# The second batch's output projection as seven block products for eight in two of three groups

## The chip, the cores and the metric

The kernel runs on one core of a Trainium2 chip. TensorE (PE) multiplies matrices, VectorE (DVE) and ScalarE (ACT) work element by element, SyncE (SP) issues the transfers. The metric is the device time of one execution in microseconds (us), the median of several. Arithmetic is float32; every weight or activation that PE sees is split into a high and a low part, and three matmuls (high x high, high x low, low x high) stand for one product.

## The reference

Two batches of 768 tokens pass through a banded attention with block summaries, and then through two layers:

```python
x = attention(q, k, v)                             # 1536 tokens x 512
x = (sigmoid(x @ w_gate) * (x @ w_val)) @ w_out    # 512 -> 1536 -> 512
h = max(x @ w1, x @ w2, x @ w3)                    # 512 -> 768
return h @ w_out2                                  # 768 -> 512
```

The change is in the product with `w_out` in the second line, for the second batch.

## The kernel before, in words

The hidden width of the first layer, 1536, is cut into 12 blocks of 128 columns (`f`), four to a group, three groups (`g`). A batch's 768 tokens are two halves of 384 (`a`), the free size of one matmul.

Batch 0 computes gate and value by plain products (`make_A`), then multiplies by `w_out` group by group (`make_B`): for each token half and each of four 128-wide output blocks (`dm`) 4 x 3 matmuls into one PSUM bank, whose sum is then copied (first group) or added (the others) to `y` in SBUF. The attention of batch 1 runs between these.

Batch 1 computes gate and value in `make_Q`, as block products: a pair of hidden blocks (`j`, six pairs), two halves of the contraction and two token halves make a 2 x 2 block product that takes seven products instead of eight (numbers 1 to 7, Strassen's scheme in Winograd's form: `FORMS` names the operand of each). A product is six matmuls of 384 columns. The weight operands are made by `blocks` (four sums on DVE) and `split` (a cast on ACT, a subtraction on DVE); the activation operands by `make_forms`. After a group's four gate and value products the projection of that group follows, by `make_B` in the plain form, 96 matmuls. The results of a group's products leave PSUM through DVE and ACT, are multiplied (gate x value) and split into the operands `h`. The second layer (`make_P`) uses block products again for both batches, and `make_D` ends the program.

The weights of batch 0 are kept in DRAM as they are converted (`keep`) and read back for batch 1 (`again`, one tile `w` of 128 x 1024 for each hidden block of `w_out`). There are ten `w` buffers, nine `h`, eight large `x`, and PSUM banks in two sets of four, `m` and `s`.

The order of every engine's instructions is made beforehand, by `Plan`: each task has an engine, a duration, a due time and the tasks that it follows; a list scheduler places them, twice refined, and the program is written in that order. The list `acc` fixes PE's order of the groups, the due times follow from it, and `chain["acc"]` keeps it.

## Time and profile before

| | |
|---|---|
| runs | 539.06, 540.60, 541.69 us; median 540.6 |
| profiled execution | 539.13 us, of which the span of its instructions is 537.4 us |
| busy share of the span | PE 98%, DVE 78%, ACT 56% |
| mean granted clock of PE | 0.997 |

Busy time is the union of an engine's instructions. Matmuls overlap, so the start of one block product to the start of the next is the better measure of PE's pace than the duration of a matmul. DVE instructions overlap a little as well. A wait is put down to whoever released it last.

### The profile page before, as it was taken

Reading aid. Unit: us, or ns where it says so; the run is one execution under the profiler, and the core shown is the slowest. Engines: PE = TensorE matmul, PEld = TensorE weight load, DVE = VectorE, ACT = ScalarE, POOL = GpSimd, SP = SyncE. Lnnn points to the kernel's source line nnn. Section 1 sums busy time; section 2 is a strip of 40 time slices with the busy share of each in tenths; the row PEclk is TensorE's granted clock in tenths of the full one; section 3 lists DMA queues with packets and bytes.
Section 4 is the critical chain, followed back from the end, with each engine's and each line's share of the span. In section 5 each row is a group of like instructions: output and inputs, shape, how many; then the busy total and the mean of one; then the engine's idle time right before and its main releaser. Section 6 shows DMA issues by size and latency. Waiting matters only on the chain.

```text
span 537.4 us, 10140 instructions
## 1 busy us (share of the span) xinstructions
PE 528.9 (98%) x3850; PEld 503.8 (94%) x3850; DVE 419.1 (78%) x988; ACT 303.5 (56%) x724; POOL 4.5 (1%) x22
## 2 busy tenths in 40 slices
PE   7999999999999999999999999999999999999997
PEld 5788999999999999999999999999999999998886
DVE  5899996999898358895389589999999998995000
ACT  5899986678656684664466167354434344463111
POOL 3000000000000000000000000000000000000000
PEclk9899999999999999999999999999999999999999
DMA  8999898969666010161143037102222223201121
GB/s 279 302 336 372 298 342 267 303 237 374 206 210 235 13 40 0 41 234 40 41 148 127 10 105 278 45 36 61 96 79 79 79 88 110 78 1 41 59 79 59
DMA packets 28128, 78.25 MB, mean 146 GB/s; under 512 B 3504, under 2 KB 6960, under 8 KB 28080
## 3 DMA queue, kind: packets, MB, share of 16 engines
q1 hardware_dynamic: 24960, 73.87, 40.5%
q10 hardware_dynamic: 3120, 3.74, 2.1%
q8 instruction: 30, 0.49, 0.4%
q14 instruction: 18, 0.15, 0.1%
HBM read 61.28 MB, written 15.73 MB: 143 GB/s over the span
## 4 chain that ended last, share of the span: by engine, by line
PE 87%; DVE 7%; DMA 2%; ACT 1%; issue 1%; SPq 1%; ACTq 0%
PE m L923 19%; PE m L884 14%; PE s L1017 12%; PE m L1017 12%; PE m L1217 9%; PE m L1116 8%; PE s L1116 8%; PE s L792 2%; DMA vn<-in_vn_dram 1%; PE s L747 1%; PE s L779 1%; DMA raw<-in_wts_dram 1%; DVE c L503 1%; DVE e L754 1%; SPq L630 1%
## 5 line engine op out<-in xcount | busy, mean ns | idle before, releaser
L884 PE MATMUL m<-x,w 128*128 128x384 f32 x576 | 108.6, 340 | 1.0 <-ACT t L901 0.8
L923 PE MATMUL m<-h,w 128*128 128x384 f32 x576 | 105.4, 336 | 0.0
L884 PEld LDWEIGHTS m<-x,w 128*128 128x128 f32 x576 | 98.7, 188 | 3.5 <-ACT t L901 1.3
L923 PEld LDWEIGHTS m<-h,w 128*128 128x128 f32 x576 | 99.6, 188 | 0.4 <-DVE y L947 0.2
L1017 PE MATMUL m<-x,w 128*128 128x384 f32 x294 | 56.1, 334 | 0.0
L1017 PE MATMUL s<-f,w 128*128 128x384 f32 x294 | 56.0, 334 | 0.0
L1017 PEld LDWEIGHTS m<-x,w 128*128 128x128 f32 x294 | 51.5, 188 | 0.1
L1017 PEld LDWEIGHTS s<-f,w 128*128 128x128 f32 x294 | 51.4, 188 | 0.1
L1116 PE MATMUL s<-f,w 128*128 128x384 f32 x252 | 48.1, 335 | 0.2 <-ACT t L1131 0.2
L1116 PE MATMUL m<-f,w 128*128 128x384 f32 x252 | 46.8, 335 | 0.0
L1116 PEld LDWEIGHTS s<-f,w 128*128 128x128 f32 x252 | 43.9, 188 | 0.6 <-ACT t L1131 0.5
L1116 PEld LDWEIGHTS m<-f,w 128*128 128x128 f32 x252 | 43.9, 188 | 0.2 <-ACT tc L1131 0.2
L760 ACT ACTIVATE e<-e,nm 128x120 f32<-128x120 f32 x96 | 36.6, 384 | 6.9 <-DVE nm L754 6.8
L435 ACT ACTIVATE w<-c 128x512 fp32r<-128x512 f32 (+1 forms) x50 | 29.3, 588 | 19.4 <-DVE c L503 12.6
L438 DVE TENSOR_TENSOR w<-raw,w 128x512 fp32r<-128x512 f32 (+1 forms) x48 | 28.6, 619 | 13.7 <-ACT w L435 13.6
L435 ACT ACTIVATE h<-t 128x384 fp32r<-128x384 f32 x48 | 24.6, 523 | 17.5 <-DVE t L1156 14.5
L499 DVE SCALAR_TENSOR_TENSOR c<-raw,c 128x512 int32<-128x512 int32 x50 | 34.2, 685 | 0.3
L503 DVE SCALAR_TENSOR_TENSOR c<-raw,c 128x512 int32<-128x512 int32 x50 | 34.1, 684 | 0.3
L435 ACT ACTIVATE w<-raw 128x512 fp32r<-128x512 f32 (+1 forms) x48 | 25.8, 571 | 14.7 <-PE m L923 11.1
L438 DVE TENSOR_TENSOR w<-c,w 128x512 fp32r<-128x512 f32 (+1 forms) x50 | 31.8, 639 | 1.9 <-ACT w L435 1.6
L438 DVE TENSOR_TENSOR h<-t,h 128x384 fp32r<-128x384 f32 x48 | 26.4, 554 | 6.6 <-ACT h L435 6.2
L1032 ACT ACTIVATE tc<-s 128x384 f32<-128x384 f32 x27 | 13.3, 491 | 27.8 <-PE s L1017 27.7
(137 smaller groups left out, 798.7 us busy)
## 6 DMA issues: line engine op xcount, KB each, us to landing
raw<-in_wts_dram SPq DMA_DIRECT2D x60, 512.0 KB, 4.2
kept_o<-w SPq DMA_DIRECT2D x12, 512.0 KB, 5.7
w<-kept_o SPq DMA_DIRECT2D x12, 512.0 KB, 5.0
k<-in_kn_dram SPq DMA_DIRECT2D x8, 400.0 KB, 7.1
q<-in_qt_dram SPq DMA_DIRECT2D x16, 192.0 KB, 6.9
v<-in_vw_dram SPq DMA_DIRECT2D x16, 192.0 KB, 5.6
raw<-kept_g SPq DMA_DIRECT2D x6, 512.0 KB, 3.1
raw<-kept_v SPq DMA_DIRECT2D x6, 512.0 KB, 4.4
```

The lines of the kernel that those rows point to most:

```text
L435: nc.scalar.activation(out=dst, in_=src, func=ACTF.Copy)
L438: nc.vector.tensor_tensor(out=dst, in0=src, in1=h.bitcast(F32), op=ALU.subtract)
L499: nc.vector.scalar_tensor_tensor(out=c.t, in0=half(r, 1), scalar=-0x40000000, in1=c.t, op0=ALU.bitwise_and, op1=ALU.bitwise_or)
L503: nc.vector.scalar_tensor_tensor(out=c.t, in0=half(r, 0), scalar=29, in1=c.t, op0=ALU.logical_shift_right, op1=ALU.bitwise_or)
L760: nc.scalar.activation(out=e[h].t[:, t], in_=e[h].t[:, t], func=ACTF.Exp, scale=-1.0, bias=nm.t[:, h, t:t + 1], accum_out=sm.t[:, h, t:t + 1])
L792: nc.tensor.matmul(px.t[64 * h:64 * h + 64, c:c + 64], lhsT=vt.t[:, t, par, h], rhs=at[h].t[0:CW, t, 64 * par:64 * par + 64], start=True, ...
L884: nc.tensor.matmul(ps.t, lhsT=w.t.rearrange("p s (k f) -> p s k f", k=KC)[:, wh, kc], rhs=src[kc // 2].t[:, xh, kc % 2], start=(kc == 0 an ...
L923: nc.tensor.matmul(ps.t, lhsT=w.t.rearrange("p s (k f) -> p s k f", k=KC)[:, wh, dm], rhs=h.t[:, xh], start=(i == 0 and j == 0), stop=(i = ...
L1017: nc.tensor.matmul(ps.t, lhsT=w.t[:, wh, c:c + 128], rhs=x.t[:, xh, kc], start=new and n == 0, stop=n == 5, skip_group_check=True)
L1032: return t, after(tag, add("ACT", 0.37, end(k), lambda: nc.scalar.activation(out=t.t, in_=ps.t, func=ACTF.Copy), [p], [t], [ps]))
L1116: nc.tensor.matmul(ps.t, lhsT=w.t[:, wh, c:c + 128], rhs=x.t[:, xh, kc], start=new and n == 0, stop=n == 5, skip_group_check=True)
L1217: nc.tensor.matmul(ps.t[:, c0:c1], lhsT=h.t[:, xh, e, c:c + 128], rhs=w.t[:, wh, c0:c1], start=(f == 0 and i == 0), stop=(f == NF2 - 1 and ...
```

## The change

In groups 1 and 2 of batch 1 the projection becomes a 2 x 2 block product as well: a pair of hidden blocks x two token halves on one side, the pair x two halves of the 512 output columns on the other. `make_E` computes its seven products, each for two column halves `m` of 128, and accumulates both pairs of the group in one bank: 7 x 2 tasks of 2 x 3 matmuls. The sums that Winograd's form shares are kept on PE's side by going on in the same bank (products 1, 6, 7 and 4), and after each of these the bank's content is added to the output (`plus`). The order of the products is 1, 3, 2, 5, 6, 7, 4.

The activation operands are made by `make_h_forms`: of a pair's four blocks (hidden block x token half) four differences on DVE and seven splits, where `done` made four splits. The odd pair's go to four large buffers `hx`. The weight operands S1 to S4 are made in the first batch's stage by `outer`, after the conversion of each odd chunk of `w_out`, and kept in DRAM; `firsts` and `again` read them back, seven tiles for a group instead of four. Of the even chunks only the first half is kept.

The plain projection of group 0 comes last: the groups run in the order 1, 2, 0. Its eight results are now added on DVE, and the first writes of the output on ACT are in group 1.

The core of the diff:

```diff
+SECOND_ORDER = (1, 2, 0)
...
+    EORDER = (1, 3, 2, 5, 6, 7, 4)
...
-    for g in range(NG):
+    second = SECOND_ORDER
+    for g in second:
...
+        if g:
+            e = [("E", g, k, m) for k in EORDER for m in range(2)]
+            acc += [e[0], ("Q", *mine[-1], 4), e[1], ("Q", *mine[-1], 3)] + e[2:]
+            continue
...
+        if nm == "S":
+            return due["E", f // 2, 5 if b == 0 else 3, 0]
+        if nm == "o" and b and f >= GF:
+            return due["E", f // GF, 2 if f % 2 else 1, 0]
...
+                n = 512 if f < GF or f % 2 else 256
+                d.k = add("SP", 1.456 * n / 512, t + KEEP, lambda: nc.sync.dma_start(
+                    out=d.t[:, :, 0:n], in_=w.t[:, :, 0:n].bitcast(F32)), [k], [d], [w])
...
+        def outer(j, t, cs):
+
+            (c0, k0), (c1, k1) = cs
+
+            def block(c, i):
+                return c.t.bitcast(F32)[:, 256 * i:256 * i + 256]
+
+            def sums(o):
+                return xs[0].t[:, 0:2].rearrange("p a b -> p (a b)")[:, 256 * o:256 * o + 256]
+
+            parts_ = (
+                (lambda: block(c0, 1), lambda: block(c1, 1), ALU.add),
+                (lambda: sums(0), lambda: block(c0, 0), ALU.subtract),
+                (lambda: block(c0, 0), lambda: block(c0, 1), ALU.subtract),
+                (lambda: block(c1, 0), lambda: sums(1), ALU.subtract))
+            fresh = "xs" not in prev
+            ks = []
+            for o, (x, y, op) in enumerate(parts_):
+                ks.append(add("DVE", 0.35, t + 1.0 + 0.4 * o, lambda o=o, x=x, y=y, op=op: nc.vector.tensor_tensor(
+                    out=sums(o), in0=x(), in1=y(), op=op), [k0, k1] + ks[-1:] + (prev.get("xs", []) if o == 0 else []),
+                    [xs[0]] if fresh and o == 0 else [], [c0, c1] + ([] if fresh and o == 0 else [xs[0]])))
+            prev["xs"] = []
+            for n in range(2):
+                h = (lambda: xs[0].t[:, 2].bitcast(F32R)) if n == 0 else (lambda: xs[1].t[:, 1])
+                l = (lambda: xs[1].t[:, 0]) if n == 0 else (lambda: xs[1].t[:, 2])
+                v = lambda n=n: xs[0].t[:, n]
+                k4 = add("ACT", 0.52, t + 3.0 + n, lambda h=h, v=v: hi(h(), v()), [ks[1 + 2 * n]],
+                         [xs[1]] if fresh and n == 0 else [], [xs[0]] + ([] if fresh and n == 0 else [xs[1]]))
+                k5 = add("DVE", 0.602, t + 3.6 + n, lambda h=h, l=l, v=v: lo(l(), v(), h()), [k4], [], xs)
+                d = kept["S", j, n] = Buf(kp, [128, 2, 512], F32, f"kept_s{j}{n}", 1)
+                a = add("SP", 0.73, t + 4.5 + n, lambda d=d, h=h: nc.sync.dma_start(
+                    out=d.t[:, 0], in_=h().bitcast(F32)), [k4], [d], xs)
+                d.k = add("SP", 0.73, t + 5 + n, lambda d=d, l=l: nc.sync.dma_start(
+                    out=d.t[:, 1], in_=l().bitcast(F32)), [k5, a], [], xs + [d])
+                prev["xs"] += [a, d.k]
...
+            if ck[1] == "o" and ck[2] >= GF:
+                if ck[2] % 2 == 0:
+                    even = c, k
+                else:
+                    outer(ck[2] // 2, t, [even, (c, k)])
+                    if even[0].tag == "cx":
+                        attention.extend(even[0].users)
...
+        def firsts(g, js, t):
+            ds = [kept["o", 2 * j] for j in js]
+            w = Buf(wp, [128, 2, 512], F32R, "w", NW)
+
+            def load():
+                for i, d in enumerate(ds):
+                    nc.sync.dma_start(out=w.t[:, :, 256 * i:256 * i + 256].bitcast(F32), in_=d.t[:, :, 0:256])
+
+            l = add("SP", 1.456, t - AGAIN, load, [d.k for d in ds], [w], ds, [prev.get("4")])
+            prev["4"] = l
+            for i, j in enumerate(js):
+                ewt[j, "A11"] = w, 256 * i, l
...
+            if nm == "S":
+                for i in range(2):
+                    ewt[f, f"S{2 * n + i + 1}"] = w, 256 * i, l
+                return
+            if f >= GF:
+                for i in range(2):
+                    ewt[f // 2, ("A12", "A22")[i]] = w, 256 * i, l
...
-            for f in range(GF * g, GF * g + GF):
-                again("o", f, first_use(1, "o", f) - WREADY)
+            if g == 0:
+                for f in range(GF):
+                    again("o", f, first_use(1, "o", f) - WREADY)
+                continue
+            js = (2 * g, 2 * g + 1)
+            firsts(g, js, first_use(1, "o", 2 * js[0]) - WREADY)
+            for n in (1, 0):
+                if n == 0:
+                    for j in js:
+                        again("o", 2 * j + 1, first_use(1, "o", 2 * j + 1) - WREADY)
+                for j in js:
+                    again("S", j, first_use(n, "S", j) - WREADY, n)
...
+    hx = [Buf(xp, [128, 2, 2, HALF], F32R, "x", 8) for _ in range(4)]
...
-        if g == 0:
+        if g == 0 and b == 0:
...
+            if j >= GF // 2:
+                held[a, e] = tb, k, at
+                return
...
+        if held:
+            make_h_forms(j, held)
+
+    def make_h_forms(j, held):
+
+        n = 0
+
+        def form(name, tb, dep, at):
+            nonlocal n
+            if j % 2 == 0:
+                h = Buf(hp, [128, 2, HALF], F32R, "h", NH)
+                part = lambda s: h.t[:, s]
+                new, uses, pre = [h], [], []
+            else:
...
+            a1 = add("ACT", 0.413, at, lambda: hi(part(0), tb.t), [dep] + pre, new, [tb] + uses)
+            if new == [h]:
+                after("h", a1)
+            elif new:
+                hxs.append(after("x", a1))
+            a2 = add("DVE", 0.469, at + 0.6, lambda: lo(part(1), tb.t, part(0)), [a1], [], [tb, h])
+            hforms[j, name] = h, part, a2
+            return a2
...
+        (W, kW, tW), (X, kX, tX), (Y, kY, tY), (Z, kZ, tZ) = (held[k] for k in ((0, 0), (1, 0), (1, 1), (0, 1)))
+        a = form("B11", W, kW, tW)
+        b_ = form("B22", Y, kY, tY)
+        c = form("B21", Z, kZ, tZ)
+        t1 = diff(W, X, W, [kX, a], tX + 0.5)
+        form("T1", W, t1, tX + 1.0)
+        t3 = diff(X, Y, X, [kY, t1], tX + 1.5)
+        t2 = diff(Y, Y, W, [t3, b_], tX + 2.0)
+        form("T2", Y, t2, tX + 2.5)
+        form("T3", X, t3, tX + 3.5)
+        n4 = diff(Z, Z, Y, [t2, c], tX + 4.0)
+        form("N4", Z, n4, tX + 4.5)
+        if j % 2:
+            past.append(j)
...
+    def make_E(g):
+        js = (2 * g, 2 * g + 1)
+        main = {}
...
+        def plus(d, m, a, ps, p, at):
+            key = a, 2 * d + m
+            if (1, *key) not in ywrite:
+                fresh = (1, d) not in ystart
+                t = add("ACT", 0.37, at, lambda: nc.scalar.activation(out=y(d, m, a), in_=ps.t, func=ACTF.Copy),
+                        [p] + ([] if fresh else [ystart[1, d]]), [yt[1, d]] if fresh else [], [ps] if fresh else [ps, yt[1, d]])
+                if fresh:
+                    ystart[1, d] = after("x", t)
+                ywrite[(1, *key)] = t
+                return t
+            t = add("DVE", 0.469, at, lambda: nc.vector.tensor_tensor(
+                out=y(d, m, a), in0=ps.t, in1=y(d, m, a), op=ALU.add), [p, ywrite[1, a, 2 * d + m]], [], [ps, yt[1, d]])
+            ywrite[1, a, 2 * d + m] = t
+            return t
+
+        for i, (k, m) in enumerate((k, m) for k in EORDER for m in range(2)):
+            wn, xn = FORMS[k]
+            new = k in (1, 2, 3, 5)
+            ps = Buf(*((ps_m, [128, HALF], F32, "m", 4) if (m + (k != 1)) % 2 == 0 else (ps_s, [128, HALF], F32, "s", 4))) if new else main[m][0]
+            dep = [] if new else [main[m][1]]
+
+            def fn(k=k, m=m, wn=wn, xn=xn, ps=ps, new=new):
+                q = 0
+                for j in js:
+                    w, c, _ = ewt[j, wn]
+                    _, part, _ = hforms[j, xn]
+                    for wh, xh in pieces:
+                        nc.tensor.matmul(
+                            ps.t, lhsT=w.t[:, wh, c + 128 * m:c + 128 * m + 128], rhs=part(xh), start=new and q == 0, stop=q == 5,
+                            skip_group_check=True)
+                        q += 1
+
+            at = due["E", g, k, m]
+            p = add("PE", 1.04, at, fn, dep + [ewt[j, wn][2] for j in js] + [hforms[j, xn][2] for j in js],
+                    [ps] if new else [], [ewt[j, wn][0] for j in js] + [hforms[j, xn][0] for j in js] + ([] if new else [ps]))
+            ptask["E", g, k, m] = p
+            for j in js:
+                eread.setdefault((j, xn), []).append(p)
+            at += 1.04
+            if k == 1:
+                main[m] = ps, plus(0, m, 0, ps, p, at)
+            elif k == 2:
+                plus(0, m, 0, ps, p, at)
+            elif k == 3:
+                plus(0, m, 1, ps, p, at)
+            elif k == 5:
+                plus(1, m, 1, ps, p, at)
+                plus(0, m, 1, ps, p, at)
+            elif k == 6:
+                main[m] = ps, plus(0, m, 1, ps, p, at)
+            elif k == 7:
+                main[m] = ps, plus(1, m, 1, ps, p, at)
+            else:
+                plus(1, m, 0, ps, p, at)
...
+    make_forms(*xf, xdone, due["Q", *pairs[0], 1] - EARLY, True, x1)
+    for n, g in enumerate(second):
+        for i, (nm, j) in enumerate(pairs[GF * n:GF * n + GF]):
+            make_Q(i, nm, j, sbuf[j % 2], GF // 2 * n + i // 2)
+        if g:
+            make_E(g)
         for x in acc:
             if x[0] == "Q" and x[2] // 2 == g:
+                after("acc", ptask[x])
+            if x[0] == "E" and x[1] == g:
                 after("acc", ptask[x])
```

What stands on PE after a group's gate and value products. `m_` and `s_` are PSUM banks, `h_` and `x_` activation operands, `w_` weight tiles; a row is three matmuls. Before, in a plain group (here the third of the second batch), a bank takes four rows with four weight tiles:

```order
L923 MATMUL m_4506<-h_4302,w_4283 128x384 x3
L923 MATMUL m_4506<-h_4262,w_4287 128x384 x3
L923 MATMUL m_4506<-h_4472,w_4297 128x384 x3
L923 MATMUL m_4506<-h_4434,w_4312 128x384 x3
L923 MATMUL m_4525<-h_4302,w_4283 128x384 x3
L923 MATMUL m_4525<-h_4262,w_4287 128x384 x3
L923 MATMUL m_4525<-h_4472,w_4297 128x384 x3
L923 MATMUL m_4525<-h_4434,w_4312 128x384 x3
```

After, the last six tasks of the first of the two groups (products 6, 7 and 4, each for two column halves):

```order
L1368 MATMUL m_3545<-h_3479,w_3513 128x384 x3
L1368 MATMUL m_3545<-x_3518,w_3528 128x384 x3
L1368 MATMUL s_3565<-h_3479,w_3513 128x384 x3
L1368 MATMUL s_3565<-x_3518,w_3528 128x384 x3
L1368 MATMUL m_3545<-h_3489,w_3428 128x384 x3
L1368 MATMUL m_3545<-x_3518,w_3438 128x384 x3
L1368 MATMUL s_3565<-h_3489,w_3428 128x384 x3
L1368 MATMUL s_3565<-x_3518,w_3438 128x384 x3
L1368 MATMUL m_3545<-h_3500,w_3451 128x384 x3
L1368 MATMUL m_3545<-x_3519,w_3510 128x384 x3
L1368 MATMUL s_3565<-h_3500,w_3451 128x384 x3
L1368 MATMUL s_3565<-x_3519,w_3510 128x384 x3
```

Two banks, `m_3545` and `s_3565`, are taken up again and again, each with one task of the other between.

The same place on DVE. `x_3550` and `x_3567` are the output `y` of the second batch, L947 adds a bank to it, L438 is the subtraction of a split and L588 a weight sum. Before, the projection of the second group:

```order
L947 TENSOR_TENSOR x_3550<-m_3927,x_3550 128x384
L438 TENSOR_TENSOR w_3982<-raw_3966,w_3982 128x512
L947 TENSOR_TENSOR x_3550<-m_3946,x_3550 128x384
L947 TENSOR_TENSOR x_3567<-m_3972,x_3567 128x384
L947 TENSOR_TENSOR x_3567<-m_3985,x_3567 128x384
L947 TENSOR_TENSOR x_3550<-m_4026,x_3550 128x384
L947 TENSOR_TENSOR x_3550<-m_4040,x_3550 128x384
L947 TENSOR_TENSOR x_3567<-m_4054,x_3567 128x384
L438 TENSOR_TENSOR w_4076<-raw_3966,w_4076 128x512
L438 TENSOR_TENSOR w_4081<-raw_3876,w_4081 128x256
L588 TENSOR_TENSOR raw_4097<-raw_3968 128x256
L947 TENSOR_TENSOR x_3567<-m_4068,x_3567 128x384
```

After, the second of the two groups. `x_3561` and `x_3650` are the output, L1351 is `plus`, L446 the subtraction of a split; `x_3519` is an operand of the projection itself, `w_4068` and `w_4081` are weights of the next group's gate product, `raw_4164` the sums for its value product:

```order
L1351 TENSOR_TENSOR x_3561<-s_4106,x_3561 128x384
L1351 TENSOR_TENSOR x_3650<-s_4106,x_3650 128x384
L1351 TENSOR_TENSOR x_3561<-m_4116,x_3561 128x384
L1351 TENSOR_TENSOR x_3650<-m_4116,x_3650 128x384
L1351 TENSOR_TENSOR x_3561<-m_4023,x_3561 128x384
L446 TENSOR_TENSOR x_3519<-t_4049,x_3519 128x384
L1351 TENSOR_TENSOR x_3561<-s_4042,x_3561 128x384
L446 TENSOR_TENSOR w_4068<-raw_3872,w_4068 128x512
L1351 TENSOR_TENSOR x_3650<-m_4023,x_3650 128x384
L446 TENSOR_TENSOR w_4081<-raw_3806,w_4081 128x256
L676 TENSOR_TENSOR raw_4164<-raw_3889 128x256
L1351 TENSOR_TENSOR x_3650<-s_4042,x_3650 128x384
```

The adds stand closer together, and weight splits for the next group stand among them that stood behind or between fewer adds.

## Rows read from the trace of the kernel before

**Rows 1.** The page: busy us (share of the span) and instructions of each engine.
```profile
PE 528.9 (98%) x3850; PEld 503.8 (94%) x3850; DVE 419.1 (78%) x988; ACT 303.5 (56%) x724; POOL 4.5 (1%) x22
```
**Rows 2.** The waits of PE: line waited for, total us, times, longest.
```profile
PE s L1279 <- DVE idle L1269: 1.2, 1, 1.2
...
PE m L884 <- ACT t L901: 0.8, 1, 0.8
...
PE s L792 <- ACT at L785: 0.2, 1, 0.2
```
**Rows 3.** Stretches: length, busy us of PE, PEld, DVE, ACT, POOL, clock, DMA share, GB/s.
```profile
214.70:260.40 45.70, 45.70 (x265) 45.70 (x265) 32.41 (x67) 25.46 (x54) 0.00 (x0) 1.00 0.27 93
260.40:307.00 46.60, 46.60 (x269) 46.25 (x268) 32.80 (x69) 22.23 (x47) 0.00 (x0) 1.00 0.26 91
307.00:353.20 46.20, 46.01 (x266) 45.69 (x265) 43.65 (x87) 27.03 (x51) 0.00 (x0) 1.00 0.39 137
353.20:482.50 129.30, 129.30 (x747) 128.94 (x746) 125.15 (x242) 56.78 (x108) 0.00 (x0) 1.00 0.22 70
...
100.00:200.00 100.00, 100.00 (x792) 95.58 (x791) 79.23 (x220) 73.14 (x194) 0.00 (x0) 1.00 0.59 201
200.00:214.70 14.70, 14.70 (x105) 14.38 (x104) 11.01 (x16) 5.74 (x9) 0.00 (x0) 1.00 0.00 1
```
**Rows 4.** PE's timeline: start, us, tile, count; in brackets idle time before.
```profile
214.69 1.20 PE L1116 MATMUL m<-f,w 128*128 128x384 f32 x6
...
219.89 1.20 PE L1116 MATMUL s<-f,w 128*128 128x384 f32 x6
220.93 3.28 PE L1116 MATMUL m<-f,w 128*128 128x384 f32 x18
...
225.09 0.68 PE L923 MATMUL m<-h,w 128*128 128x384 f32 x3
...
260.45 1.20 PE L1116 MATMUL m<-f,w 128*128 128x384 f32 x6
...
271.04 0.68 PE L923 MATMUL m<-h,w 128*128 128x384 f32 x3
...
307.03 1.20 PE L1116 MATMUL m<-f,w 128*128 128x384 f32 x6
...
353.25 1.20 PE L1017 MATMUL s<-f,w 128*128 128x384 f32 x6
```
**Rows 5.** DVE's timeline, the same columns.
```profile
225.81 0.56 DVE L947 TENSOR_TENSOR y<-m,y 128x384 f32<-128x384 f32 x1 [0.23 <-PE m L923]
...
229.22 0.69 DVE L438 TENSOR_TENSOR w<-raw,w 128x512 fp32r<-128x512 f32 x1
229.82 0.42 DVE L588 TENSOR_TENSOR raw<-raw 128x256 f32<-128x256 f32 x1
...
234.15 0.55 DVE L438 TENSOR_TENSOR h<-t,h 128x384 fp32r<-128x384 f32 x1
234.62 0.42 DVE L438 TENSOR_TENSOR w<-raw,w 128x256 fp32r<-128x256 f32 x1
...
260.27 1.74 DVE L438 TENSOR_TENSOR w<-raw,w 128x512 fp32r<-128x512 f32 x3 [9.74 <-ACT w L435]
...
269.23 0.56 DVE L1155 TENSOR_TENSOR t<-m,t 128x384 f32<-128x384 f32 x1 [2.12 <-PE m L1116]
269.82 0.56 DVE L1156 TENSOR_TENSOR t<-t,x 128x384 f32<-128x384 f32 x1
```
**Rows 6.** Groups of instructions: line, operation, shapes, count, busy us, mean ns, idle before.
```profile
L435 ACT ACTIVATE h<-t 128x384 fp32r<-128x384 f32 x48 | 24.6, 523 | 17.5 <-DVE t L1156 14.5 <-DVE t L906 2.1 <-DVE t L1168 0.7
L438 DVE TENSOR_TENSOR h<-t,h 128x384 fp32r<-128x384 f32 x48 | 26.4, 554 | 6.6 <-ACT h L435 6.2
L947 DVE TENSOR_TENSOR x<-m,x 128x384 f32<-128x384 f32 x16 | 8.9, 554 | 5.9 <-PE m L923 5.9
```
**Rows 7.** Tile `kept_o`: us from issue to landing, of stores and reads together.
```profile
DMA to landing us min/median/max: 4.2/5.3/7.8
```

More of the change, by code (lines that the diff above doesn't have):

```diff
@@ L423 @@
         due[x] = at
-        at += 6 * 0.68 if x[0] == "D" else 1.04 if x[0] in "PQ" or len(x) == 5 else 2.08
+        at += 6 * 0.68 if x[0] == "D" else 1.04 if x[0] in "PQE" or len(x) == 5 else 2.08
     UPB = len(units) // B
-    m2 = due["Q", "g", 0, 1] - EARLY
+    m2 = due["Q", *pairs[0], 1] - EARLY
     target = {}
@@ L530, in keep @@
                 d = kept[nm, f] = Buf(kp, [128, 2, 512], F32, f"kept_o{f}", 1)
-                d.k = add("SP", 1.456, t + KEEP, lambda: nc.sync.dma_start(
-                    out=d.t, in_=w.t.bitcast(F32)), [k], [d], [w])
+                n = 512 if f < GF or f % 2 else 256
+                d.k = add("SP", 1.456 * n / 512, t + KEEP, lambda: nc.sync.dma_start(
+                    out=d.t[:, :, 0:n], in_=w.t[:, :, 0:n].bitcast(F32)), [k], [d], [w])
                 return
@@ L539, in keep @@
             d.k = k
+        xs = [Buf(xp, [128, 3, 512], F32 if i == 0 else F32R, "x", 8) for i in range(2)]
+        def outer(j, t, cs):
[29 more added lines that the diff above has]
+                prev["xs"] += [a, d.k]
         for ck in chunks:
@@ L554, in again @@
             prev["4"] = l
+            if nm == "S":
[5 more added lines that the diff above has]
+                    ewt[f // 2, ("A12", "A22")[i]] = w, 256 * i, l
             wt[1, nm, f], wready[1, nm, f] = w, l
-        for g in range(NG):
-            for nm, j in pairs[GF * g:GF * g + GF]:
+        for i, g in enumerate(second):
+            for nm, j in pairs[GF * i:GF * i + GF]:
                 t = due["Q", nm, j, 1] - WREADY
@@ L942, in make_B @@
             k = add("ACT", 0.37, end, lambda: nc.scalar.activation(out=y(), in_=ps.t, func=ACTF.Copy),
-                    [l] + ([] if first else [ystart[at]]), [yb] if first else [], [ps] if first else [ps, yb])
+                    [l] + ([] if first else [ystart[at]]), [yb] if first else [],
+                    [ps] if first else [ps, yb])
             if first:
-                ystart[at] = k if b == 0 else after("x", k)
+                ystart[at] = k
         else:
@@ L1146, in joined @@
             if gate:
-                fresh = (a, e) == (0, 0) and j < 2
+                fresh = (a, e) == (0, 0) and q < 2
                 k = add("DVE", 0.469, at, lambda: nc.vector.tensor_tensor(out=view(a, e), in0=ps.t, in1=tb.t, op=ALU.add),
-                        p + ([] if fresh else sread[j - 2] + [swrite[j % 2]]), [s] if fresh else [], [tb, ps] + ([] if fresh else [s]))
+                        p + ([] if fresh else sread[q - 2] + [swrite[q % 2]]), [s] if fresh else [], [tb, ps] + ([] if fresh else [s]))
                 if fresh:
-                    swrite[j] = after("x", k)
+                    swrite[q] = after("x", k)
                 sready[j, a, e] = add("ACT", 0.371, at + 0.8, lambda: nc.scalar.activation(
@@ L1164, in direct @@
                 sready[j, a, e] = add("ACT", 0.371, at, lambda: nc.scalar.activation(
-                    out=view(a, e), in_=ps.t, func=ACTF.Sigmoid), [p, swrite[j % 2]] + sread[j - 2], [], [s, ps], tab="S")
+                    out=view(a, e), in_=ps.t, func=ACTF.Sigmoid), [p, swrite[q % 2]] + sread[q - 2], [], [s, ps], tab="S")
                 return
@@ L1169, in direct @@
                 out=tb.t, in0=ps.t, in1=view(a, e), op=ALU.mult), [p, sready[j, a, e]], [tb], [ps, s]))
-            sread[j].append(k)
+            sread[q].append(k)
             done(a, e, tb, k, at + 0.6)
+        held = {}
         A, Bk, Ck = banks
@@ L1187, in make_Q, with diff @@
         joined(1, 0, c2, Ck, [p3, k2], end(3))
+        if held:
[9 more added lines that the diff above has]
+            else:
+                h, i = hx[n // 2], n % 2
+                part = lambda s: h.t[:, i, s]
+                new, uses, pre = [], [h], eread.get((past[-1], name), []) if past else []
+                if not past and n == 0:
+                    new, uses = hx, []
+                elif not past:
+                    pre = pre + [hxs[0]]
+                n += 1
+            a1 = add("ACT", 0.413, at, lambda: hi(part(0), tb.t), [dep] + pre, new, [tb] + uses)
[6 more added lines that the diff above has]
+            return a2
+        def diff(out, x, y, dep, at):
+            return add("DVE", 0.469, at, lambda: nc.vector.tensor_tensor(out=out.t, in0=x.t, in1=y.t, op=ALU.subtract),
+                       dep, [], [out, x, y])
+        (W, kW, tW), (X, kX, tX), (Y, kY, tY), (Z, kZ, tZ) = (held[k] for k in ((0, 0), (1, 0), (1, 1), (0, 1)))
[12 more added lines that the diff above has]
+            past.append(j)
@@ L1241 @@
                 make_B(0, g, a, dm)
-    make_forms(*xf, xdone, due["Q", "g", 0, 1] - EARLY, True, x1)
-    for g in range(NG):
-        for i, (nm, j) in enumerate(pairs[GF * g:GF * g + GF]):
-            make_Q(i, nm, j, sbuf[j % 2])
+    make_forms(*xf, xdone, due["Q", *pairs[0], 1] - EARLY, True, x1)
[4 more added lines that the diff above has]
+            make_E(g)
         for x in acc:
             if x[0] == "Q" and x[2] // 2 == g:
+                after("acc", ptask[x])
+            if x[0] == "E" and x[1] == g:
                 after("acc", ptask[x])
```

15 lines of the change are left out of this document (9 added, 6 removed).

## The prediction

> **What bounds the kernel now.** I read the busy shares first. PE is busy for 98% of the span, DVE for 78% and ACT for 56% [rows 1]. Next I read who waited for whom, for PE: there are eight, from 1.2 us down to 0.2, and together 5 us; the one at 0.8 us is on line 884, the first layer of batch 0 [rows 2]. From about 80 us to 500 us PE has work without a visible break. So an edit pays only by taking matmuls away from PE, and it costs whatever makes PE wait.
>
> Then the stage that is changed, by the table of stretches: the three groups of the second batch, from 214.7 to 353.2 us [rows 3]. PE is full in each (45.70 of 45.70, 46.60 of 46.60, 46.01 of 46.20). DVE is busy 32.41, 32.80 and 43.65 us. In the next stage, the 129.30 us of the second layer's block products, DVE is busy 125.15 us, 97%, and PE still never idles. DVE is the second bound and nearly equal there; in the changed groups it has 13.3, 13.8 and 2.6 us left.
>
> PE's own timeline gives the pace: a block product of six 384-column matmuls starts 1.04 us after the one before, 0.173 us a matmul [rows 4]. A group has 28 such products and 96 matmuls of the projection, 264 in all, which is 45.8 us at that pace. The groups begin at 214.69, 260.45, 307.03 and the next stage at 353.25, so they last 45.76, 46.58 and 46.22 us. The second carries three matmuls of the group before (271.04), 0.5 us; what is left over pace is 0.0, 0.3 and 0.5 us. That is what short waits cost a group today; only 0.19 us of it shows as idle.
>
> **The change, part by part.** *PE.* In groups 1 and 2 the projection takes 7 products x 2 column halves x 2 pairs x 3 matmuls = 84 instead of 96. That is 24 matmuls fewer, 24 x 0.1733 = 4.16 us, all on the path, since PE is full there.
>
> The Trainium skill (TensorE: Matmul & The Clock Gate, Back-to-back issue gap) puts an isolated gap at columns divided by 2.4 GHz plus 2.5 ns, 162.5 ns here. By it the saving would be 3.9 us. The row's 173 ns is measured in this stage, so it decides.
>
> *DVE in groups 1 and 2.* Each pair of hidden blocks now makes seven split operands instead of four, and four differences: 3 + 4 = 7 more DVE instructions, 14 a group. Each group has 16 evictions instead of 8. In the first of the three, 8 of them are copies on ACT, as all 8 were before, so 8 more fall on DVE; in the second all 16 are DVE adds for 8 before. So 22 more DVE instructions of 384 columns in each of the two groups. The group's row says 554 ns for one [rows 6], but they overlap: starts are 0.47 us apart (234.15, 234.62), and 0.59 where the second needs the first (269.23, 269.82) [rows 5]. 22 x 0.47 = 10.3 us. DVE then has 32.41 + 10.3 = 42.7 us in 45.8 - 2.1 = 43.7 us, 98%, and 32.80 + 10.3 = 43.1 in 44.5, 97%. The third group keeps its 8 adds and stays at 94%. Since DVE at 97% cost PE no idle time in the next stage [rows 3], I take no cost for the load as such. The bounds: 0, and at 0.59 us each 22 x 0.12 = 2.6 us more a group, less about 1 us that is free, 1.6 us late a group.
>
> *The chain of one bank.* Products 6, 7 and 4 accumulate in one bank, with an add to the output after each, and only the other column half, 1.04 us, stands between two of them. An add starts 0.20 us after its matmuls are issued (PE's 225.09 plus three matmuls, DVE's 225.81) and takes 0.56 [rows 4, 5]. With 0.1 us to release PE that is 0.86 of 1.04 us: it fits if DVE is free. Is it? From the end of the last block product to the second half of product 4, PE has 11 blocks, 11.4 us; less 0.20 and 0.1, DVE has 11.1 us. By the order of the changed kernel 23 DVE instructions stand there: in the second of the two groups 20 of 384 columns, one of 512 and two of 256, 20 x 0.47 + 0.60 + 2 x 0.34 = 10.7 us (0.60 from 229.22 to 229.82; 0.34 is the 0.42 of a 256-column one less the same 0.08 of overlap [rows 5]); in the first 17, two and four, 10.6 us. Two dependent neighbours add 0.24. About 0.2 us is left, so I expect waits of some tenths, like those the groups have now: 0.3 us a group, 0.6 us in all, the middle of the 0.0 to 0.5 above. The bounds are 0 and, at full 0.554 us each, 20 x 0.085 = 1.7 less 0.4, 1.3 us a group.
>
> Does it matter that 16 of the new adds read PSUM? An add from PSUM takes 554 ns and a split from SBUF 554 ns [rows 6]. The Trainium skill (Perfetto Trace Analysis, Optimizing Scalar/DVE Operations) gives DVE a larger access overhead on PSUM, about 125 against 60 ns. By it the 16 adds would need 1.0 us more and the chain would be late. The two equal rows speak against it; the late chain is the first rival below, on other grounds.
>
> *ACT.* Six more casts a group, 6 x 0.523 us = 3.1 us at full duration [rows 6], on 25.46 and 22.23 us of about 45 [rows 3]. Free.
>
> *The weight sums* (S1 to S4 of the output matrix) are made in the first batch's stage: for 4 pairs four sums of 256 columns and two splits of 512 on DVE, 16 x 0.34 + 8 x 0.60 = 10.2 us. DVE is busy 79.23 of the 100 us from 100 to 200, and 11.01 of the next 14.7 [rows 3]: 24 us are free, and PE waits on nothing there [rows 2]. Cost 0; if all of it fell late, the next group's operands would be 10.2 - 3.7 = 6.5 us behind, which I keep for the upper end only.
>
> *Transfers.* Seven weight tiles are read back for a group instead of four. Such a read lands in 4.2 to 7.8 us [rows 7]. By the order the last one is issued about ten products, 10 us, before its use. SP issues them in turn behind the raw weights of the next group; the share of the DMA engines is 0.27 there [rows 3]. Cost 0, at most 3 us if one lands in 7.8 us after waiting behind three others.
>
> *The order of the groups.* The plain group comes last. It hands the second layer its input as before, with the same 8 adds. Cost 0. Below nothing: no other PE work goes away, so the gain has 4.2 us as its end.
>
> **Sum.** The profiled execution took 539.13 us (span 537.4, 1.7 us around it). 539.13 - 4.16 + 0.6 = 535.6. It lies 1.5 us under the median of the three runs, 540.6, so against that median the forecast is 540.6 - 3.6 = 537.0 us. A measurement tells 0.5%, 2.7 us, from no change: under 537.9 is faster, over 543.3 slower.
>
> **Rivals.** *First: DVE sets the pace in the block stretch.* The chain of 23 instructions has 0.2 us to spare, and DVE stands at 97 to 98% of both groups. Late by 1.3 us a group (full durations) the sum is 540.6 - 4.16 + 2.6 = 539.0; at the dependent pace, 20 x 0.12 - 0.4 = 2.0 a group, 540.4. For it: PE lost up to 0.5 us in groups with less on DVE. Against: the next stage, 97% without idle. Chance 0.29, and it ends within 0.5%.
>
> *Second, slower: the next group's weights come late.* The seven tiles take seven of the ten weight buffers, so the splits for the next group's first product move into the block stretch, behind its adds, as the order shows. Before, DVE had 9.74 us of idle time in that place [rows 5]. If DVE is late there, the first product also waits for its whole weight block: four sums and four splits, 4 x 0.34 + 3 x 0.60 + 0.34 = 3.5 us. At two boundaries that is 7.0 us, and with the 0.6: 540.6 - 4.16 + 7.6 = 544.0 us. It decides as soon as the last split of that block ends after the group's last projection matmul. For it: the third group, the fullest on DVE, has the only idle time of the stage, 0.19 us [rows 3]. Against: the order puts all but the last parts of that block before the end of the stretch. Chance 0.10.
>
> *Third: the saving is whole, without any wait:* 540.6 - 4.2 = 536.4. It lies inside the forecast's own range. That the matmuls do not go away is no rival: the count follows from the loops.
>
> **How the numbers follow.** The forecast with the third has 0.61, own range 535.3 to 538.3 (the three runs lie within 1.5 us of their median); the first rival 0.29; the second 0.10. Faster by over 0.5%: 0.58, since a little of the forecast's range lies above 537.9. Slower: 0.09. Same: 0.33. The range for 8 in 10 runs from 535.2 to 540.8: it takes in the first rival whole and leaves the second out.
>
> **What would show it.** Right: the second batch's stage 138.5 us long before and about 135 after; the two groups near 44 us and the plain one near 46; DVE over 95% busy in the first two; PE's visible waits in the block stretches under 1 us; 24 matmuls fewer. The first rival shows as idle time of PE, or stretched products, at the second halves of products 7 and 4, released by DVE's adds. The second shows as waits of the next group's first product on a DVE split. The forecast is wrong if the two groups last 45.5 us or more, or if the first stage or the next one has grown by over a microsecond.

## The result, and the profile after

The changed kernel takes 535.92 us (median; 535.43 to 536.01), the kernel before 540.81 beside it: ratio 0.991, 95% interval 0.989 to 0.994, so 4.9 us less (3.2 to 5.9 by the interval). The forecast was 537.0. Timed once more it came out the same (run e8 below, 0.992).

The page of the changed kernel, its line of busy shares, against [rows 1]:

```profile
PE 523.4 (98%) x3826; PEld 499.3 (93%) x3826; DVE 447.2 (84%) x1056; ACT 313.1 (59%) x744; POOL 4.5 (1%) x22
```

TensorE (PE) has 24 matmuls fewer. VectorE (DVE) has 68 instructions and 28 us of work more, ScalarE (ACT) 10 us. How this went in each stretch is seen in the table of stretches of the changed kernel, the columns of [rows 3]; the first two are the groups with seven products, the third the plain group, the last the block products of the second layer:

```profile
216.50:260.60 44.10, 43.93 (x253) 43.57 (x253) 41.37 (x86) 26.84 (x56) 0.00 (x0) 1.00 0.39 132
260.60:304.50 43.90, 43.90 (x254) 43.70 (x253) 40.20 (x85) 23.63 (x50) 0.00 (x0) 1.00 0.35 120
304.50:350.30 45.80, 45.80 (x266) 45.70 (x265) 44.41 (x89) 27.43 (x53) 0.00 (x0) 1.00 0.44 150
350.30:479.00 128.70, 128.70 (x745) 128.70 (x744) 126.55 (x248) 58.10 (x110) 0.00 (x0) 1.00 0.23 70
```

The borders are read from PE's timeline of the changed kernel, as in [rows 4] (start, us, tile, count, idle time before). L1206 are the block products, L1368 the seven products, L1107 the next stage:

```profile
216.49 1.20 PE L1206 MATMUL m<-f,w 128*128 128x384 f32 x6
...
256.37 0.79 PE L1368 MATMUL m<-h,w 128*128 128x384 f32 x3 [0.17 <-DVE x L1351]
...
260.68 1.20 PE L1206 MATMUL m<-f,w 128*128 128x384 f32 x6
...
304.55 1.20 PE L1206 MATMUL m<-f,w 128*128 128x384 f32 x6
...
350.36 1.20 PE L1107 MATMUL s<-f,w 128*128 128x384 f32 x6
```

The groups last 44.19, 43.87 and 45.81 us; the stage 133.87. Before, it was 138.56, of which 0.52 are three matmuls of the first batch (225.09 in [rows 4]) that now run ahead of it: 138.04 to 133.87 is 4.17 us less, which the interval of the timed ratio takes in. From there to the span's end it is 184.15 us before (537.4 - 353.25) and 183.84 after (534.2 - 350.36). The first stage ends 1.80 us later: 0.52 are those three matmuls, and PE waited longer for the first loads than the 1.0 us before (the waits of PE, whole span, changed kernel):

```profile
PE s L744 <- DMA vn<-in_vn_dram: 3.1, 3, 1.4
...
PE m L1368 <- DVE x L1351: 0.2, 1, 0.2
```

The second of these rows is the one visible wait of PE from 216 to 479 us.

### The profile page after: what moved, and what is told of

The parts are those of the page before. It is cut to its first block, busy times and chain, and to the rows that moved or that the text cites. A ratio compares the mean times of both kernels' runs of the same rounds, so it can differ in the third digit from the quotient of the medians.

```text
span 534.2 us, 10243 instructions
## 1 busy us (share of the span) xinstructions
PE 523.4 (98%) x3826; PEld 499.3 (93%) x3826; DVE 447.2 (84%) x1056; ACT 313.1 (59%) x744; POOL 4.5 (1%) x22
## 4 chain that ended last, share of the span: by engine, by line
PE 85%; DVE 4%; ACT 4%; DMA 4%; issue 1%; SPq 1%; ACTq 0%
PE m L972 14%; PE m L1012 13%; PE m L1107 12%; PE s L1107 12%; PE m L1424 9%; PE s L1206 8%; PE m L1206 8%; DMA vn<-in_vn_dram 3%; PE m L1368 2%; PE s L1368 2%; PE s L880 1%; DMA raw<-in_wts_dram 1%; PE s L867 1%; SPq L718 1%; PE s L835 1%
## 5 line engine op out<-in xcount | busy, mean ns | idle before, releaser
L1012 PE MATMUL m<-h,w 128*128 128x384 f32 x384 | 70.8, 338 | 0.0
L1012 PEld LDWEIGHTS m<-h,w 128*128 128x128 f32 x384 | 66.2, 188 | 0.4 <-DVE c L511 0.2
L1107 PE MATMUL m<-x,w 128*128 128x384 f32 x294 | 56.1, 334 | 0.0
L1107 PE MATMUL s<-f,w 128*128 128x384 f32 x294 | 56.0, 334 | 0.0
L1107 PEld LDWEIGHTS m<-x,w 128*128 128x128 f32 x294 | 51.5, 188 | 0.1
L1107 PEld LDWEIGHTS s<-f,w 128*128 128x128 f32 x294 | 51.4, 188 | 0.0
L1206 PE MATMUL s<-f,w 128*128 128x384 f32 x252 | 47.6, 334 | 0.0
L1206 PE MATMUL m<-f,w 128*128 128x384 f32 x252 | 46.6, 335 | 0.0
L1206 PEld LDWEIGHTS s<-f,w 128*128 128x128 f32 x252 | 44.0, 188 | 0.1
L1206 PEld LDWEIGHTS m<-f,w 128*128 128x128 f32 x252 | 43.9, 188 | 0.0
L446 DVE TENSOR_TENSOR w<-c,w 128x512 fp32r<-128x512 f32 (+1 forms) x50 | 31.7, 638 | 1.9 <-ACT w L443 1.8
L446 DVE TENSOR_TENSOR w<-raw,w 128x512 fp32r<-128x512 f32 (+1 forms) x48 | 28.9, 620 | 2.2 <-ACT w L443 2.0
L446 DVE TENSOR_TENSOR h<-t,h 128x384 fp32r<-128x384 f32 x46 | 24.9, 551 | 6.8 <-ACT h L443 6.8
L1434 ACT ACTIVATE c<-m 128x512 f32<-128x512 f32 (+1 forms) x13 | 7.3, 565 | 38.9 <-PE m L1424 38.9
L443 ACT ACTIVATE h<-t 128x384 fp32r<-128x384 f32 x46 | 23.2, 520 | 7.7 <-DVE t L1249 3.2
```

The costliest lines, as they stand in the source:

```text
L443: nc.scalar.activation(out=dst, in_=src, func=ACTF.Copy)
L446: nc.vector.tensor_tensor(out=dst, in0=src, in1=h.bitcast(F32), op=ALU.subtract)
L1012: nc.tensor.matmul(ps.t, lhsT=w.t.rearrange("p s (k f) -> p s k f", k=KC)[:, wh, dm], rhs=h.t[:, xh], start=(i == 0 and j == 0), stop=(i = ...
L1107: nc.tensor.matmul(ps.t, lhsT=w.t[:, wh, c:c + 128], rhs=x.t[:, xh, kc], start=new and n == 0, stop=n == 5, skip_group_check=True)
L1206: nc.tensor.matmul(ps.t, lhsT=w.t[:, wh, c:c + 128], rhs=x.t[:, xh, kc], start=new and n == 0, stop=n == 5, skip_group_check=True)
L1434: nc.scalar.activation(out=o.t[:, c0:c1], in_=ps.t[:, c0:c1], func=ACTF.Copy)
```

## The experiments

In all runs "stage" is the time from the second batch's first block product to the next stage's first, less 0.52 us for each three matmuls of the first batch that fall into it. It repeats to 0.04 us between the two profiles of the changed kernel, while the stage ahead of it ends anywhere from 214.7 to 218.7 us, so sizes are read from the stage and the timed ratio is a check on them. A group is counted from its first block product to the next group's first, with all that PE runs between: in e4's first group three matmuls of the first batch (0.52 us), in e9's six (1.04 us). "Over pace" is what a group lasts beyond 0.1733 us for each of its matmuls.

| kernel | ratio to before, 95% | groups as they run, us | stage, us |
|---|---|---|---|
| before | | 45.76, 46.58, 46.22 | 138.04 |
| changed | 0.991 (0.989 to 0.994) | 44.19, 43.87, 45.81 | 133.87 |
| e8 changed, again | 0.992 (0.990 to 0.994) | 44.19, 43.83, 45.81 | 133.83 |
| e1 matmuls put back | 0.999 (0.997 to 1.001) | 45.96, 45.92, 45.81 | 137.69 |
| e2 order alone | 1.000 (0.999 to 1.001) | 45.76, 46.59, 46.22 | 138.05 |
| e3 seven in one group | 0.998 (0.996 to 1.000) | 44.27, 45.76, 46.23 | 136.26 |
| e4 seven in all three | 1.006 (1.004 to 1.008) | 45.08, 44.82, 51.53 | 140.91 |
| e5 DVE work at the chain | 1.001 (0.999 to 1.003) | 46.00, 47.40, 45.81 | 139.21 |
| e6 DVE work ahead of it | 1.000 (0.998 to 1.001) | 46.14, 45.68, 45.81 | 137.63 |
| e7 product 6 early | 0.998 (0.997 to 1.000) | 44.86, 44.93, 46.23 | 136.02 |
| e9 differences on GpSimd | 0.998 (0.996 to 0.999) | 47.47, 44.36, 45.82 | 136.61 |
| e10 half of e5, one group | 0.994 (0.993 to 0.996) | 44.20, 44.90, 45.81 | 134.91 |

**e1.** Product 2's matmuls run twice:
```
-                q = 0
-                for j in js: ...
+                for _ in range(2 if k == 2 else 1):
+                    q = 0
+                    for j in js: ...
```


> The changed kernel in which the six matmuls of each half of product 2 are run twice in both groups (24 matmuls in all, 12 a group), the second time over the first, so that the values stay what they were. VectorE's and ScalarE's work, the transfers and the order of the groups are those of the changed kernel. Theory (the gain is the 24 matmuls that TensorE no longer runs, at 0.173 us each): the time goes back by 4.2 us, to 540.1 us against 535.9 of the changed kernel, ratio to the kernel before 0.997 to 1.000. Rival 1 (the gain comes from the order of the groups or the other work laid beside them): the time stays within 1 us of 535.9, ratio 0.991 to 0.993. Rival 2 (VectorE sets the pace of the two groups, and hides part of the matmuls): the time goes back by less than 4.2 us, by 2 to 3 us, since the twelve matmuls give VectorE 2.1 us of room in each group.

The stage goes back by 3.82 us, the time to that of before. PE's timeline of this run, the starts of the three groups and of the next stage:

```profile
216.94 1.20 PE L1206 MATMUL m<-f,w 128*128 128x384 f32 x6
...
262.90 1.20 PE L1206 MATMUL m<-f,w 128*128 128x384 f32 x6
...
308.82 1.20 PE L1206 MATMUL m<-f,w 128*128 128x384 f32 x6
...
354.63 1.20 PE L1107 MATMUL s<-f,w 128*128 128x384 f32 x6
```

45.96 and 45.92 us are PE's pace for 264 matmuls (45.76) and 0.2 more. With all the new DVE work in place the gain is gone: it was the matmuls. The 0.34 us short of 4.16 is what twelve more matmuls a group give back in waits (0.51 and 0.19 us over pace before, 0.20 and 0.16 now).

**e2 and e3.** A set names the groups with seven products; empty, or group 1 alone:
```
+BLOCKED = ()          # e3: (1,)
-        if g:
+        if g in BLOCKED:
...
```


> The order of the three groups of the changed kernel (1, 2, 0), with all three as eight products. Theory: 24 matmuls stay, so the time is that of the kernel before within 0.8 us: ratio 0.9985 to 1.0015. Rival (the order carries a part of the gain, by laying the heavy group at another place of the stage): 2 us or more faster than before, ratio 0.996 or less; or slower, in which case the seven products have given more than 4.9 us.

> Seven products in group 1 alone, the other two groups as eight products, order 1, 2, 0. Theory (12 matmuls less at 0.173 us): 2.1 us less than the kernel before, 538.7 us, ratio 0.995 to 0.997. Rival (the gain is not in proportion: the first of the two groups pays the weight sums and the fill, the second harvests): 0 to 1 us less, ratio 0.998 to 1.000; or nearly all of the gain, ratio below 0.994.

The order does nothing: the groups of e2 are those of before to 0.01 us. One group gives 1.78 us of the stage for 2.08 of matmuls, and the group itself lasts 0.59 over pace, much as group 1 does in the changed kernel (0.51). The timed ratio, 0.998, is a little short of the 0.995 to 0.997 expected, with an interval that reaches into it.

**e4.** The same set with (0, 1, 2).

> Seven products in all three groups, order 1, 2, 0. TensorE has 12 matmuls less again, VectorE some 22 instructions more in the third group, where it was busy for 44.4 of 45.8 us. Theory (there VectorE has no room: 44.4 + 10.3 = 54.7 us of work in a group that TensorE would finish in 43.7 us): the third group becomes VectorE's, up to 9 us longer, so 5 to 9 us slower than the changed kernel, unless part of that work moves into neighbouring stretches; 538 us is the least that this theory takes. Rival (the work is spread over free time elsewhere, and VectorE's share in a group means nothing): 2.1 us less than the changed kernel, 533.8 us, ratio 0.987.

The third group becomes DVE's, as the theory has it: DVE is busy for 49.41 us in a group that PE could finish in 43.68. Stretches of this run, the third group whole and two parts of it, and PE's and DVE's timelines there:

```profile
304.90:356.50 51.60, 47.55 (x255) 45.74 (x254) 49.41 (x102) 26.28 (x53) 0.00 (x0) 0.93 0.41 143
...
347.90:349.00 1.10, 1.10 (x3) 1.10 (x4) 1.10 (x3) 0.32 (x1) 0.00 (x0) 0.50 0.82 108
...
351.00:353.50 2.50, 2.46 (x8) 2.47 (x9) 1.51 (x4) 0.00 (x0) 0.00 (x0) 0.50 0.00 0
```
```profile
347.90 1.01 PE L1369 MATMUL m<-x,w 128*128 128x384 f32 x2 [3.30 <-DVE x L447]
```
```profile
342.96 0.42 DVE L677 TENSOR_TENSOR S<-c 128x256 f32<-128x256 f32 x1
...
346.96 0.42 DVE L447 TENSOR_TENSOR w<-c,w 128x256 fp32r<-128x256 f32 x1
347.30 0.55 DVE L447 TENSOR_TENSOR x<-t,x 128x384 fp32r<-128x384 f32 x1
```

PE waits 3.30 us for a split on DVE (347.30), and behind that wait its granted clock is 0.50, the lower of its two levels (1.2 GHz), until 353.5. Of the 7.85 us that the group lasts over pace, 3.3 are this wait and 3.0 the 32 matmuls behind it (8.59 us for 5.55); the rest lies in shorter waits ahead. On DVE the split stands behind eight instructions that prepare weights of the second layer (from 342.96 on). Whether another order of DVE's work would have spared PE a part of the wait was not tried. Group 0 was left plain to good effect: against the changed kernel all three cost 7.0 us in the stage, 5.7 of them in the third group.

**e5, e6 and e10.** The same DVE work, at two places and in two amounts:
```
+            many = 5 if j % 2 == 1 and name == "N4" else 1     # e6: j % 2 == 0 and name == "T1"
+                                                               # e10: 3 if j == 5 and name == "N4"
-            a2 = add("DVE", 0.469, at + 0.6, lambda: lo(part(1), tb.t, part(0)), ...
+            a2 = add("DVE", 0.469, at + 0.6, lambda: [lo(part(1), tb.t, part(0)) for _ in range(many)], ...
```


> The changed kernel with one VectorE instruction of the second pair of blocks (the split of its last form, N4, 128x384) run five times for once in each of the two groups: 4 x 0.47 = 1.88 us more VectorE work a group, values unchanged. It stands directly ahead of the adds of the product 6, for whose bank product 7 waits. Theory (the chain of one bank is tight by a few tenths of a us, and VectorE idles 0.47 us there): in group 1 TensorE waits 1.2 to 1.6 us at the first half of product 7, in group 2 between 0.8 and 1.6 us; the time is 2 to 3.2 us above the changed kernel, 538 to 539 us. Rival (VectorE has 6% to 8% of free time in the groups, 2.7 and 3.7 us, and takes the work into it wherever it stands): within 0.6 us of the changed kernel.

DVE's timeline of e5 (the repeated split) in group 2, and PE's in both groups:

```profile
301.37 2.92 DVE L446 TENSOR_TENSOR x<-t,x 128x384 fp32r<-128x384 f32 x5
304.21 0.55 DVE L1352 TENSOR_TENSOR x<-s,x 128x384 f32<-128x384 f32 x1
```
```profile
257.90 0.79 PE L1369 MATMUL m<-h,w 128*128 128x384 f32 x3 [1.98 <-DVE x L1352]
...
302.26 0.69 PE L1369 MATMUL m<-x,w 128*128 128x384 f32 x3
304.81 0.79 PE L1369 MATMUL s<-h,w 128*128 128x384 f32 x3 [1.87 <-DVE x L1352]
305.44 1.12 PE L1369 MATMUL s<-x,w 128*128 128x384 f32 x3
...
309.09 0.68 PE L1369 MATMUL s<-x,w 128*128 128x384 f32 x3
```

The amount added was larger than the 1.88 us intended. The repeated splits write the same tile; five of them take 2.92 us where one takes 0.55, so they start 0.59 us apart, like the two neighbours in [rows 5] of which one needs the other, and not 0.47. That is 2.37 us more in each group.

The wait is where the theory puts it, at product 7 behind product 6's add, but larger: 1.98 us (0.17 of it was there before) and 1.87, and the time is 541.2 us where 538 to 539 was expected. Not all of the 2.37 us came back. Group 1 loses 1.81 us, since DVE's idle time ahead of the bank's adds (0.47 us in the changed kernel) took a part. In group 2 product 7's second half starts 2.03 us late (0.52 after 302.26 would be in time), so 0.34 us was spare there. Group 2 loses 3.53 us in all: the wait, and 12 matmuls that take 3.65 us (305.44 to 309.09) for 2.08.

> The run with extra VectorE work at the chain, made smaller: the split of form N4 three times for once (2 x 0.47 = 0.94 us more) and in the second of the two groups alone. There the earlier run had a wait of 1.87 us of TensorE, after which the granted clock was 0.54 for 3.7 us, so that the group lasted 3.5 us longer. Theory (the wait is the extra work itself less what the chain has to spare, and the clock falls only after a longer wait): TensorE waits 0.8 to 1.0 us at the second half of product 7, the granted clock stays at 1.0, the group lasts 44.7 to 45.0 us for 43.87. Rival (any visible wait there costs the clock too): the group lasts 46 us or more, with a granted clock below 0.9 behind the wait.

DVE's and PE's timelines of e10 there, and the stretch behind it:

```profile
301.29 1.73 DVE L446 TENSOR_TENSOR x<-t,x 128x384 fp32r<-128x384 f32 x3
```
```profile
302.18 0.69 PE L1369 MATMUL m<-x,w 128*128 128x384 f32 x3
303.55 0.79 PE L1369 MATMUL s<-h,w 128*128 128x384 f32 x3 [0.68 <-DVE x L1352]
```
```profile
305.00:307.00 2.00, 2.00 (x12) 1.74 (x11) 2.00 (x5) 0.00 (x0) 0.00 (x0) 1.00 0.00 0
```

Three splits take 1.73 us for 0.55, so 1.18 us were added. Product 7's second half starts 0.85 us late (303.55, for 302.18 and 0.52), again 0.33 less than what was added; 0.68 of it shows as idle time, less than the 0.8 to 1.0 expected. The group is 1.03 us longer, within the range expected, and the clock stays at 1.00. So the chain's price, without a loss of clock, is about 0.9 us for each us of DVE work.

> The same 4 x 0.47 us more VectorE work in each of the two groups, but at the split of form T1 of the first pair of blocks, 13 to 19 us ahead of the bank's chain, while TensorE is still at the blocks' own products. Theory (VectorE's idle moments between there and the chain, 0.26 + 0.28 + 0.27 + 0.35 + 0.37 + 0.37 us in the rows of group 1, take it): 0 to 0.6 us above the changed kernel. Rival (VectorE sets the pace of the groups as a whole, or its queue is served late everywhere): the same loss as with the extra work at the chain, 2 to 3.2 us.

Here the theory fails. The groups last 1.95 and 1.81 us longer (44.19 to 46.14, 43.87 to 45.68), most of the 2.37 us added (2.92 for 0.55 again), though it stands 13 us and more ahead of the bank's chain. The loss of 3.76 us in the stage is even above the rival's 2 to 3.2, but the rival's mechanism, DVE as the pace of whole groups, is not what PE's waits show: the new ones stand in the block products alone. DVE's, ACT's and PE's timelines of e6 in group 1:

```profile
236.31 2.92 DVE L446 TENSOR_TENSOR h<-t,h 128x384 fp32r<-128x384 f32 x5
239.16 0.55 DVE L1241 TENSOR_TENSOR x<-m,tc 128x384 f32<-128x384 f32 x1
```
```profile
239.74 0.53 ACT L1245 ACTIVATE x<-x 128x384 f32<-128x384 f32 x1 [1.79 <-DVE x L1241]
...
243.78 0.47 ACT L1221 ACTIVATE t<-s 128x384 f32<-128x384 f32 x1
```
```profile
239.76 1.32 PE L1206 MATMUL m<-f,w 128*128 128x384 f32 x6 [0.26 <-DVE x L1241]
...
244.30 1.31 PE L1206 MATMUL s<-f,w 128*128 128x384 f32 x6 [1.13 <-ACT t L1221]
```

The join of the block products (L1241, a DVE sum of two products), queued behind the splits on DVE, is late; ACT waits for it 1.79 us, comes late to its own eviction (L1221), and that holds the bank that PE wants. The block products have a chain of their own, and in group 1 of the changed kernel DVE has less than half a microsecond of idle time from 223.0 to 242.4 us (18.93 us busy of 19.40); its idle time comes later, where DVE itself waits for PE or ACT.

**e7.** `EORDER = (1, 3, 2, 6, 5, 7, 4)`.

> The changed kernel with product 6 run ahead of product 5 in both groups (1, 3, 2, 6, 5, 7, 4), so that two tasks of TensorE (2.1 us) lie between product 6 and the product 7 that adds to its bank. Theory (the chain of the bank costs what the groups last beyond TensorE's pace, 0.51 and 0.19 us): 0.2 to 0.6 us less than the changed kernel. Rival (that excess is not the chain's): no difference, within 0.2 us; or a loss, when the adds of product 5, two for each half, now come between product 7's bank and the next use.

Slower by 2.15 us in the stage, where the theory had 0.2 to 0.6 us less: PE's waits at product 7 are gone, but it waits 0.41 and 0.40 us for splits instead. With two waits of 0.19 for ACT, one in group 1 and one in the plain group, that is 1.2 of the 2.15; the rest lies in stretched matmuls and wasn't taken apart.

**e8.** The changed kernel, unedited.

> The changed kernel itself once more, as a yardstick beside the next two on the same chip. Expected from its first four times: ratio to the kernel before 0.989 to 0.994. Rival (a part of the 4.9 us was the start of those runs, whose first stage waited for transfers by 1 to 3 us more or less from run to run): 0.994 to 0.996, that is 2 to 3 us.

The first theory holds.

**e9.** The first pair's differences on GpSimd:
```
-            return add("DVE", 0.469, at, lambda: nc.vector.tensor_tensor(...
+            eng, cost, to = ("POOL", 0.9, nc.gpsimd) if j % 2 == 0 else ("DVE", 0.469, nc.vector)
+            return add(eng, cost, at, lambda: to.tensor_tensor(...
```


> The changed kernel with the four form differences of the first pair of blocks in each of the two groups (128x384, L1314) on GpSimd in place of VectorE: 4 x 0.47 = 1.88 us less VectorE work a group. GpSimd has not run such an instruction in any trace here. Theory (the groups last 44.19 and 43.87 us, and TensorE's pace is 252 x 0.1733 = 43.68: VectorE can give back at most the difference): at most 0.7 us less than the changed kernel in the stage of the second batch. Rival 1 (what sits on the chain is the length of a difference, not VectorE's load; GpSimd is slower for each): the forms come later, and each group lasts 0.5 to 3 us longer. Rival 2 (VectorE's load of 92% to 94% is what the groups last): 1 us or more a group less, which TensorE's pace forbids.

Slower by 2.7 us in the stage: 2.2 in group 1 (47.47 less 1.04, for 44.19) and 0.5 in group 2. That is the size that the first rival gave, but PE waits for none of the forms; in group 1 it waits 0.61 us for the join (L1241), 0.94 for ACT behind it and 0.17 at product 7, as in the changed kernel. GpSimd's and DVE's timelines of this run:

```profile
235.69 3.73 POOL L1315 TENSOR_TENSOR t<-t 128x384 f32<-128x384 f32 x3 [229.72 <-DVE t L1249]
239.99 1.18 POOL L1315 TENSOR_TENSOR t<-t 128x384 f32<-128x384 f32 x1 [0.56 <-DVE h L446]
```
```profile
235.90 2.66 DVE L446 TENSOR_TENSOR w<-raw,w 128x512 fp32r<-128x512 f32 x2
238.48 1.83 DVE L446 TENSOR_TENSOR h<-t,h 128x384 fp32r<-128x384 f32 x2
240.24 0.54 DVE L1241 TENSOR_TENSOR x<-m,tc 128x384 f32<-128x384 f32 x1
```

While GpSimd runs its differences (1162 ns each), two DVE splits take 2.66 us that take 1.29 elsewhere in the changed kernel, and the next two 1.83 for 1.03. The join behind them is late as in e6. The Trainium skill (SBUF — State Buffer, Who interferes with whom) says that a DVE instruction with two SBUF inputs contends with a GpSimd instruction that reads SBUF; these rows agree, and the join at 240.24, which takes one input from PSUM, lasts its usual time (0.54 us) beside the fourth difference. The planner also laid some other work differently here, so not all of the 2.7 us is shown to be this.

No version here beats the changed kernel.

## Why the prediction was right, and where its steps were off

**PE, 24 matmuls, 4.16 us on the path: right.** The count fell by 24, the stage by 4.17 us, e1 brings 3.82 of it back, and e2 leaves nothing to the order (predicted 0).

**The chain of one bank, 0.3 us a group: right in place, and in size for both groups together.** The two groups last 0.51 and 0.19 us over pace (252 x 0.1733 = 43.68), 0.70 for 0.6 predicted, and the one visible wait is at product 7 behind product 6's add, in group 1. DVE's timeline of the changed kernel there:

```profile
254.96 0.56 DVE L1351 TENSOR_TENSOR x<-m,x 128x384 f32<-128x384 f32 x1 [0.47 <-ACT x L1345]
255.44 0.41 DVE L446 TENSOR_TENSOR w<-raw,w 128x256 fp32r<-128x256 f32 x1
255.77 0.55 DVE L1351 TENSOR_TENSOR x<-m,x 128x384 f32<-128x384 f32 x1
```

PE's 256.37 starts 0.05 us after the add of 255.77 ends (the sum allowed 0.1). "About 0.2 us is left" comes near what e5 and e10 show at product 7's second half in group 2, 0.33 us. But in group 1 DVE is not the only one in the chain: ahead of 254.96 it idles for 0.47 us, put down to a copy on ACT (L1345), one of those that write the output for the first time and stand in group 1 alone. ACT's load was free, as predicted; whether these copies are why group 1 lasts 0.51 over pace and group 2 only 0.19 was not tested.

**The sum added the 0.6 us to what the groups lost before: there it is 0.6 too high.** They lost 0.0, 0.3 and 0.5 us over pace; now 0.51, 0.19 and 0.05. The new waits came in place of the old. In before, e2 and e3 a plain group behind another plain one lasts 0.3 to 0.5 us over pace, and a plain one behind seven products 0.0 in e3 and 0.05 in the changed kernel; e7 breaks the pattern (46.23), and its cause was not looked for. This is the term that was mis-sized: 3.6 us predicted, 4.17 in the stage.

**DVE at 98 and 97%: it is 94 and 92%** (41.37 of 44.10, 40.20 of 43.90), below the 95% named as a sign; the work grew by 9.0 and 7.4 us, not 10.3. By window, differences, splits and adds came to 8 + 6 + 7 = 21 more of 384 columns, as counted but for one, but the planner moved 2 and 5 weight and input preparations out of the two groups: 19 and 16 more instructions in all (67 to 86, 69 to 85).

**No cost for the load as such: right in the result, wrong in the reason.** The reason was that DVE at 97% does not hold PE up in the next stage. e6 shows that of 2.37 us of extra work 1.95 and 1.81 come back as time, although 2.7 and 3.7 us of the groups are idle on DVE. The 9.0 and 7.4 us fitted; most of another 2.4 did not. That PE was not idle in the next stage said nothing about what was left here.

**The first rival was close.** Its mechanism, with its place, is what e5 shows, and its price of 1 to 2 us a group needs only some 2 us more on DVE. **The second rival did not come:** no wait of PE stands at a group's start. **Weight sums, transfers, ACT: 0, right;** with half as many sums again, e4 starts the second batch at 215.06 us, and e2, with none, at 215.57, so the 1.28 us by which the changed kernel's first stage was later is not theirs. It had been named as a sign against the forecast; as the start of this program varies by more, it was a poor one.

**Adds from PSUM cost what splits from SBUF cost.** The groups of instructions of the changed kernel bear out [rows 6]:

```profile
L446 DVE TENSOR_TENSOR x<-t,x 128x384 fp32r<-128x384 f32 x14 | 7.7, 552 | 0.3
...
L1351 DVE TENSOR_TENSOR x<-s,x 128x384 f32<-128x384 f32 x12 | 6.6, 554 | 0.1
```
